# Reading the values' PSUM bank twice on ScalarE and making x's low part on Pool, in units 1 to 7

## The chip, the cores and the metric

The kernel runs on one core of a Trainium2 chip. The metric is the device time of one execution in microseconds (us), from the first to the last instruction with what lies around them; the profile gives the span of one execution, engine by engine.

## What is computed

Three blocks follow each other. Attention takes q, k and v of 4 batches, 8 heads, 768 positions and 64 values a head; every query sees 8 global keys and 96 local ones, with a bias that grows with the distance. Its output is laid out as x, 3072 tokens by 512. The first feed-forward block is dense, the second sends each token to one of eight experts. Cut to what matters here:

```python
attn_out = softmax(scale * q @ k.T + bias, masked) @ v
x = attn_out.transpose(0, 2, 1, 3).reshape(B * S, H * D)   # 3072 x 512
h = x @ w_in                                               # 512 x 2048
z = (h * cos(h)) @ w_out                                   # 2048 x 512
out = z, or for tokens with z @ w_skip > 0: z + gate * expert(z)
```

## The kernel before

**Units.** The 3072 tokens are eight units of 384 (UT), numbered 0 to 7. For each unit attention gives x transposed: four chunks of 128 rows (one pair of heads each, `p` = 0 to 3) by 384 tokens. The dense block needs x more exactly than one rounded operand, so x is held as two fp32r tiles, `xhi` (x rounded) and `xlo` (what is left), and each product is three matmuls: `wi_hi` by `xhi`, `wi_hi` by `xlo`, `wi_lo` by `xhi` (L516). The second product, `zp` (L555), does the same with `ghi`, `glo`, `wo_hi` and `wo_lo`.

**What runs beside what.** The attention of unit 0 comes first (up to about 53 us). After that `unit(u)` runs the dense block of unit u in 16 steps `f`, and the attention of unit u+1 is dealt out over its 32 slots (two a step, `HS`). Through unit 0's dense block the weights are converted as well (L212 to L264). In units 1 to 6 the first half of the slots also holds the routing scores of the unit before: 27 products on VectorE (DVE), `junk` L613. Unit 7 has no attention beside it; the experts follow.

**One pair of heads in the slots.** With s0 the first slot of pair p, scores come at s0, s0+1 and s0+2 (`att_S`, t = 0, 1, 2: two matmuls each into two PSUM banks `ps_s`, L394, each read by DVE at L399, which adds the bias and gives the minimum). The exponentials (L413, ScalarE) follow, then the scaling by Pool (L423), the transposes `ps_p` at s0+5 to s0+7 (copied out by ScalarE, L439 and L441, into `pT`), and at s0+9 the product with the values, `ps_v` (`att_V`, L450 and L455). As pairs are eight slots apart, `att_V` of one pair stands in the same slot as `att_S` t = 1 of the next, just ahead of it; t = 2 is one slot later.

**The banks.** From unit 1 on, `ps_s`, `ps_p` and `ps_v` take turns in three banks of the pool `ps_a` (one tag). Around `att_V` the turn is: `ps_v` in the first bank, the two products of t = 1 in the second and third, then the two products of t = 2 in the first (which `ps_v` must have left) and in the second (which L399 of t = 1, first head, must have read). In unit 0 the values' product is in a bank of another pool (`hp`).

**The values' bank before.** ScalarE rounds it into `xhi` (L464); DVE then reads it again and subtracts `xhi` (L465) to make `xlo`. The bank is free when L465 is done.

**Order on the engines.** TensorE's and ScalarE's instructions run in the order in which the program states them. DVE's and Pool's order is chosen by the framework's planner from its own estimates when the program is built, and each engine then keeps that order whatever is late. ScalarE's order in a step is: L488 (rounds the angle of `hp`), in an `att_V` step L464, then L504 (the sine, which waits for DVE's L499), then L526 (`ghi`). DVE's is L499, L542 (`r` times `hp`), L482 (`wi_lo`) with the attention's and the routing's work between. Pool makes `wi_hi` (L479) and `glo` (L527), and in unit 0's dense block also L230 of the conversion.

**The tile that the change takes.** `pT` has three buffers (`HT`), one for each t of a pair; they are read by the matmuls of `att_V`.

Of the kernel before, what the change touches and what calls it, by code (L numbers as in the profile page):

```python
# [9 lines left out]
F32 = mybir.dt.float32  # L10
# [5 lines left out]
ALU = mybir.AluOpType  # L16
# [4 lines left out]
P = 128  # L21
# [16 lines left out]
def kernel(  # L38
    ctx, tc, q, k, v, n_global, n_local, w_in, w_out, w_skip, w_gate, w1, w2, out
):  # L40
    nc = tc.nc
# [8 lines left out]
    HT = 3  # L50
    UT = HT * P
# [20 lines left out]
    ap_ = att_pool.enter_context(tc.tile_pool(name="ap", bufs=2))  # L72
# [12 lines left out]
        out=upper, in_=ones, pattern=[[1, P]], base=0, channel_multiplier=-1,  # L85
# [15 lines left out]
    for j, a in enumerate((n_global, n_local)):  # L101
# [11 lines left out]
        out=lim, in0=lim_h, scalar=2.0 ** 32, in1=lim, op0=ALU.mult, op1=ALU.add  # L113
# [19 lines left out]
        out=loc, in0=rel, scalar=nlo, in1=dst, op0=ALU.is_lt, op1=ALU.mult  # L133
# [14 lines left out]
    def to_far(d, kept):  # L148
# [12 lines left out]
        out=dst_f, in0=tmp, scalar=nlo, in1=dst[:, 104:NW], op0=ALU.mult, op1=ALU.add  # L161
# [6 lines left out]
        out=dst[:, 0:8], in0=g8[:, 0:8], scalar1=nlo, scalar2=None, op0=ALU.mult  # L168
# [170 lines left out]
    def att_ps(u, name):  # L339
        if u == 0:  # L340
            if name == "ps_v":
                return ps_h.tile([P, UT], F32, name="hp")
            return ps_z.tile([P, DM], F32, name="zp")
        return ps_a.tile([P, 512], F32, name=name, tag="ps")
# [98 lines left out]
    def att_V(u, p):  # L443
        d = att[u, p]
        av = att_ps(u, "ps_v")
        for t in range(HT):
            first, pt = u % 2 == 0 and t == 0, d["pt", t]
            if not first:
                for j in range(2):
                    nc.tensor.matmul(  # L450
                        av[j * D:(j + 1) * D, t * P:(t + 1) * P], d["va"][:, t, j, :],
                        pt[0:104, 0, j, :], start=True, stop=False,
                    )
            for j in range(2):
                nc.tensor.matmul(  # L455
                    av[j * D:(j + 1) * D, t * P:(t + 1) * P], d["v"][:, t, j, :],
                    pt[:, 1, j, :], start=first, stop=True,
                )
        if p == 0:
            att[u, "x"] = (  # L460
                mp.tile([P, CC, UT], F32R, name="xhi"), mp.tile([P, CC, UT], F32R, name="xlo")
            )
        xhi, xlo = att[u, "x"]
        nc.scalar.copy(xhi[:, p], av[:, 0:UT])  # L464
        nc.vector.tensor_tensor(  # L465
            out=xlo[:, p], in0=av[:, 0:UT], in1=xhi[:, p].bitcast(F32), op=ALU.subtract
        )


    gq = {}  # L470
# [251 lines left out]
    for u in range(1, NU):  # L722
        for p in range(NP):
            s0 = HS * (u - 1) + PS * p - 3
            at(s0 - 12, att_load, u, p)
            at(s0 - 5, att_load_v, u, p)
            at(s0 - 5, att_Tq, u, p)
            at(s0 - 4, att_Tk, u, p)
            for t in range(HT):
                at(s0 + t, att_S, u, p, t)  # L730
                at(s0 + 5 + t, att_P, u, p, t)
            at(s0 + 9, att_V, u, p)
            at(s0 + 2, att_load_va, u, p)
            at(s0 + 2, att_E, u, p, tail=True)
# [33 lines left out]
    for p in range(NP + 1):  # L768
        if p < NP:
            if p > 1:  # L770
                att_load_v(0, p)
            for t in range(HT):
                att_S(0, p, t)
            if p + 1 < NP:
                att_Tq(0, p + 1)
                att_Tk(0, p + 1)
            if p + 1 < NP:
                fill(p + 1)
            if p + 2 < NP:
                att_load(0, p + 2)  # L780
            att_E(0, p)
        warm(2, ps_a, "ps")
        if p > 0:
            for t in range(HT):
                att_P(0, p - 1, t)
            att_V(0, p - 1)
            if p < NP:
                att_load_va(0, p)
        conv_tick()
# [168 lines left out]
    with tc.manual_schedule(engines={mybir.EngineType.PE}):  # L958
# [8 lines left out]
        with tc.manual_schedule(engines={mybir.EngineType.SP}):  # L967
            with tc.manual_schedule(engines={mybir.EngineType.Activation}):


                u = NU - 1
# [72 lines left out]
                with tc.manual_schedule(engines={mybir.EngineType.Pool, mybir.EngineType.DVE}):  # L1044
                    with tc.manual_schedule(engines={mybir.EngineType.Activation}):
# [17 lines left out]
                        def trans_x0(cs):  # L1063
# [16 lines left out]
                            out=sel, in0=slots, scalar1=r.sf[:, 0], scalar2=None, op0=ALU.is_equal  # L1080
# [67 lines left out]
        out=ctl[:, 1:2], in0=ctl[:, 4:5], scalar1=float(NE), scalar2=None, op0=ALU.is_gt  # L1148
# [207 lines left out]
    with tc.If(reg(ctl_i[0:1, 1:2], 1) > 0):  # L1356
# [4 lines left out]
        with tc.tile_pool(name="gp", bufs=2) as gp:  # L1361
# [9 lines left out]
                out=nb[:, 0:E], in0=nb[:, 0:E], scalar1=1.0 / P,  # L1371
# [3 lines left out]
                out=nb[:, E:E + 1], in0=ctl[:, 0:1], scalar1=-float(NB0), scalar2=float(NB0),  # L1375
# [6 lines left out]
            for e in range(E):  # L1382
                nc.gpsimd.indirect_dma_start(
                    out=xs[:, :], out_offset=bass.IndirectOffsetOnAxis(ap=pi[:, e:e + 1], axis=0),
# [40 lines left out]
```

## Time and profile before

| | |
|---|---|
| runs, us | 1033.59, 1036.96, 1031.6 (median 1033.59) |
| profiled execution, us | 1035.09 |
| its span, us | 1033.3 |
| PE busy | 967.6 us, 94% |
| DVE busy | 740.2 us, 72% |
| Pool busy | 539.7 us, 52% |
| ScalarE busy | 528.2 us, 51% |
| mean granted TensorE clock | 0.967 |

Busy time is a sum over the whole span. A row of a timeline gives start, duration, engine, line and names; what stands in brackets is the idle time of that engine just before it and the instruction that ended it. PE is the matmul row, PEld the weight loads, ACT is ScalarE, POOL is Pool. One matmul of fp32 operands shows as two records.

### The profile page before, as it was taken

Reading aid. Unit: us, or ns where it says so; the run is one execution under the profiler, and the core shown is the slowest. Engines: PE = TensorE matmul, PEld = TensorE weight load, DVE = VectorE, ACT = ScalarE, POOL = GpSimd, SP = SyncE. Lnnn points to the kernel's source line nnn. Section 1 sums busy time; section 2 is a strip of 40 time slices with the busy share of each in tenths; the row PEclk is TensorE's granted clock in tenths of the full one; section 3 lists DMA queues with packets and bytes.
Section 4 is the critical chain, followed back from the end, with each engine's and each line's share of the span. In section 5 each row is a group of like instructions: output and inputs, shape, how many; then the busy total and the mean of one; then the engine's idle time right before and its main releaser. Section 6 shows DMA issues by size and latency. Waiting matters only on the chain.

```text
span 1033.3 us, 17028 instructions
## 1 busy us (share of the span) xinstructions
PE 967.6 (94%) x5673; PEld 814.5 (79%) x5677; DVE 740.2 (72%) x1835; ACT 528.2 (51%) x1279; POOL 539.7 (52%) x727
## 2 busy tenths in 40 slices
PE   8888888999999999999899999999999999999996
PEld 4577666878787887788788778877898789999995
DVE  6588887896698569658854975696474288888883
ACT  4676766656556565566576566656564111111110
POOL 3577767443454444454455445454555165656662
PEclk8889889999999999999999999999999989999998
DMA  7386764544554321122111211200004187556500
GB/s 184 88 228 181 209 179 148 162 120 138 144 142 132 103 63 28 34 54 69 28 40 40 58 28 41 67 12 17 12 31 181 37 322 267 198 203 222 196 25 21
DMA packets 141824, 115.07 MB, mean 111 GB/s; under 512 B 99735, under 2 KB 116119, under 8 KB 141600
## 3 DMA queue, kind: packets, MB, share of 16 engines
q1 hardware_dynamic: 138496, 107.89, 34.9%
q0 software_dynamic: 3200, 5.98, 1.5%
q8 instruction: 47, 0.77, 0.3%
q14 instruction: 49, 0.40, 0.1%
q10 hardware_dynamic: 32, 0.03, 0.0%
HBM read 97.36 MB, written 21.05 MB: 115 GB/s over the span
## 4 chain that ended last, share of the span: by engine, by line
PE 53%; DVE 25%; POOL 10%; issue 6%; ACT 3%; DMA 2%; POOLq 0%; SPq 0%; ACTq 0%; DVEq 0%
PE hp L516 13%; PE zp L555 13%; PE hp L933 9%; PE zp L952 9%; DVE junk L613 8%; DVE wi_lo L482 4%; POOL sc L423 4%; PE ps_s L394 3%; POOL wi_hi L479 2%; DVE r L499 2%; POOL glo L527 2%; DVE sc L399 2%; DVE r L542 2%; DVE w_in_sb L219 1%; DVE w_in_sb L223 1%
## 5 line engine op out<-in xcount | busy, mean ns | idle before, releaser
L527 POOL TENSOR_TENSOR glo<-r,ghi 128x384 fp32r<-128x384 f32 x115 | 130.9, 1138 | 198.1 <-ACT ghi L526 178.5
L516 PE MATMUL hp<-xhi,wi_hi 128*128 128x384 f32 x492 | 179.2, 364 | 4.6 <-DVE r L542 3.1
L482 DVE TENSOR_TENSOR wi_lo<-w_in_sb,wi_hi 128x512 fp32r<-128x512 f32 x124 | 108.0, 871 | 102.8 <-POOL wi_hi L479 100.2
L516 PE MATMUL hp<-xhi,wi_lo 128*128 128x384 f32 x492 | 168.5, 342 | 1.1 <-DVE wi_lo L482 1.1
L516 PE MATMUL hp<-xlo,wi_hi 128*128 128x384 f32 x492 | 168.0, 342 | 0.0
L555 PE MATMUL zp<-wo_hi,ghi 128*128 128x512 f32 x345 | 147.4, 427 | 0.4 <-ACT r_zr L575 0.4
L504 ACT ACTIVATE r<-r,halfpi 128x384 f32<-128x384 f32 x128 | 78.9, 617 | 132.9 <-DVE r L499 131.7
L555 PE MATMUL zp<-wo_lo,ghi 128*128 128x512 f32 x345 | 137.2, 398 | 3.9 <-DVE wo_lo L264 3.9
L613 DVE CUSTOM_DVE_ANT_0 junk<-r_zr,wrep 128x512 bf16<-128x512 f32 x162 | 135.5, 837 | 7.1 <-ACT r_zr L575 5.3
L555 PE MATMUL zp<-wo_hi,glo 128*128 128x512 f32 x345 | 136.8, 397 | 0.1
L423 POOL TENSOR_SCALAR sc<-sc,sm 128x232 f32<-128x232 f32 (+1 forms) x180 | 88.8, 513 | 70.1 <-DVE sm L418 59.1
L526 ACT CAST ghi<-r 128x384 fp32r<-128x384 f32 x115 | 59.0, 513 | 108.2 <-DVE r L542 107.6
L516 PEld LDWEIGHTS hp<-xhi,wi_hi 128*128 128x128 f32 x492 | 94.6, 192 | 20.0 <-issue 14.1
L479 POOL TENSOR_SCALAR wi_hi<-w_in_sb 128x512 fp32r<-128x512 f32 x128 | 92.0, 719 | 33.0 <-PE hp L516 26.1
L394 PE MATMUL ps_s<-kW,qT 64*128 64x232 f32 (+1 forms) x384 | 81.1, 415 | 27.7 <-DVE xlo L465 14.7
L938 ACT ACTIVATE hh<-hp 128x256 fp32r<-128x256 f32 x64 | 24.7, 386 | 149.3 <-PE hp L933 149.3
L516 PEld LDWEIGHTS hp<-xhi,wi_lo 128*128 128x128 f32 x492 | 94.4, 192 | 1.5 <-DVE wi_lo L482 1.4
L516 PEld LDWEIGHTS hp<-xlo,wi_hi 128*128 128x128 f32 x492 | 94.8, 193 | 0.2
L394 PEld LDWEIGHTS ps_s<-kW,qT 64*128 64x128 f32 x384 | 42.8, 197 | 62.0 <-DVE xlo L465 21.3
L413 ACT ACTIVATE sc<-sc,mx 128x232 f32<-128x232 f32 (+1 forms) x180 | 83.3, 464 | 6.1 <-DVE mx L399 4.8
L542 DVE TENSOR_TENSOR r<-r,hp 128x384 f32<-128x384 f32 x112 | 61.5, 549 | 31.6 <-ACT r L504 31.4
L871 POOL TENSOR_SCALAR w2h<-we 128x512 fp32r<-128x512 f32 x64 | 48.7, 760 | 67.3 <-PE zp L952 67.3
(234 smaller groups left out, 2266.6 us busy)
## 6 DMA issues: line engine op xcount, KB each, us to landing
we<-in_moe_w_dram SPq DMA_DIRECT2D x16, 2048.0 KB
st<-in_moe_w_in_dram SPq DMA_DIRECT2D x16, 512.0 KB
st<-in_moe_w_out_dram SPq DMA_DIRECT2D x16, 512.0 KB
ck<-in_moe_w_in_dram SPq DMA_DIRECT2D x16, 512.0 KB
ck<-in_moe_w_out_dram SPq DMA_DIRECT2D x16, 512.0 KB
ld_q<-in_q_dram SPq DMA_DIRECT2D x64, 96.0 KB
ld_k<-in_k_dram SPq DMA_DIRECT2D x64, 96.0 KB
ld_v<-in_v_dram SPq DMA_DIRECT2D x64, 96.0 KB
```

The costliest lines, as they stand in the source:

```text
L394: nc.tensor.matmul(sp[:, c0:NW], d["qT"][j * D:(j + 1) * D, t * P:(t + 1) * P], d["kW"][j * D:(j + 1) * D, t, c0:NW], start=True, stop=True,)
L413: nc.scalar.activation(out=s[:, j, c0:NW], in_=s[:, j, c0:NW], func=AF.Exp, scale=-1.0, bias=d["m"][:, t, j:j + 1], accum_out=sm[:, t, j:j ...
L423: nc.gpsimd.tensor_scalar(out=s[:, j, c0:NW], in0=s[:, j, c0:NW], scalar1=sm[:, t, j:j + 1], scalar2=1.0, op0=ALU.mult, op1=ALU.mult,)
L479: nc.gpsimd.tensor_scalar(out=hi, in0=ws, scalar1=1.0, scalar2=1.0, op0=ALU.mult, op1=ALU.mult)
L482: eng.tensor_tensor(out=lo, in0=ws, in1=hi.bitcast(F32), op=ALU.subtract)
L516: nc.tensor.matmul(hp, a[:, c, :], b[:, c, :], start=(n == 0), stop=(n == 3 * CC - 1))
L527: nc.gpsimd.tensor_tensor(out=glo, in0=r, in1=ghi.bitcast(F32), op=ALU.subtract)
L542: nc.vector.tensor_tensor(out=r, in0=r, in1=hp, op=ALU.mult)
L555: nc.tensor.matmul(zt[u][t], a[:, sl], b[:, f, :], start=(f == 0 and n == 0), stop=(f == FC - 1 and n == 2),)
L613: nc.vector.tensor_tensor_reduce(out=junk, in0=self.zr[:, t, 0:DM], in1=self.wrep[e], op0=ALU.mult, op1=ALU.add, scale=1.0, scalar=0.0, ac ...
L933: nc.tensor.matmul(hp, a[:, c, :], b[:, c, :], start=(n == 0), stop=(n == 3 * CC - 1))
L952: nc.tensor.matmul(yq[e][j], a[:, sl], b, start=(f == 0 and n == 0), stop=(f == F2C - 1 and n == 2),)
```

## The change

In units 1 to 7 ScalarE reads the values' bank a second time and copies it as it is into a new tile `xf`, which is taken from the buffers of `pT`. Pool subtracts `xhi` from `xf` to make `xlo`. In unit 0 all stays.

```diff
         xhi, xlo = att[u, "x"]
         nc.scalar.copy(xhi[:, p], av[:, 0:UT])
-        nc.vector.tensor_tensor(
-            out=xlo[:, p], in0=av[:, 0:UT], in1=xhi[:, p].bitcast(F32), op=ALU.subtract
-        )
+        if u == 0:
+            nc.vector.tensor_tensor(
+                out=xlo[:, p], in0=av[:, 0:UT], in1=xhi[:, p].bitcast(F32), op=ALU.subtract
+            )
+        else:
+
+            xf = ap_.tile([P, 2, 2, P], F32, name="pT", bufs=HT)
+            xf = xf.rearrange("p a b c -> p (a b c)")[:, 0:UT]
+            nc.scalar.copy(xf, av[:, 0:UT])
+            nc.gpsimd.tensor_tensor(out=xlo[:, p], in0=xf, in1=xhi[:, p].bitcast(F32), op=ALU.subtract)
```

## Rows read from the trace of the kernel before

**Rows 1.** The page, busy time of each engine and its share of the span.
```profile
PE 967.6 (94%) x5673; PEld 814.5 (79%) x5677; DVE 740.2 (72%) x1835; ACT 528.2 (51%) x1279; POOL 539.7 (52%) x727
```
**Rows 2.** Busy time by stretch: length, PE, PEld, DVE, ACT, POOL, then clock, DMA.
```profile
70.00:162.00 92.00, 78.18 (x404) 63.02 (x402) 76.17 (x133) 60.67 (x139) 68.82 (x72) 0.89 0.67 189
...
540.00:634.00 94.00, 90.64 (x542) 76.14 (x541) 66.28 (x199) 58.33 (x143) 45.91 (x69) 1.00 0.17 42
...
573.00:583.00 10.00, 9.41 (x63) 7.54 (x62) 9.46 (x30) 5.04 (x11) 3.92 (x4) 1.00 0.14 32
```
**Rows 3.** DVE's read of the values' bank, and TensorE's wait for the bank.
```profile
L465 DVE TENSOR_TENSOR xlo<-ps_v,xhi x28: 543/551/554, 77.4 to 742.9; 128x384 fp32r<-128x384 f32 x28
...
PE ps_s L394: 14.7, 14
```
**Rows 4.** Waits, units 1 to 6 (162 to 729 us): total, times, longest.
```profile
POOL glo L527 <- ACT ghi L526: 174.2, 66, 5.6
...
ACT r L504 <- DVE r L499: 91.9, 59, 3.3
...
PE ps_s L394 <- DVE xlo L465: 10.4, 11, 1.2
```
**Rows 5.** Waits, unit 0's dense block (70 to 162 us): total, times, longest.
```profile
PE ps_s L394 <- DVE xlo L465: 4.3, 3, 3.3
```
**Rows 6.** Timeline around one stop of TensorE in unit 5.
```profile
574.35 1.25 POOL L527 TENSOR_TENSOR glo<-r,ghi 128x384 fp32r<-128x384 f32 x1 [4.05 <-PE hp L516]
...
574.78 1.37 DVE L613 CUSTOM_DVE_ANT_0 junk<-r_zr,wrep 128x512 bf16<-128x512 f32 x1
...
575.44 0.66 PE L394 MATMUL ps_s<-kW,qT 64*128 64x232 f32 x4
...
575.56 0.48 ACT L464 CAST xhi<-ps_v 128x384 fp32r<-128x384 f32 x1 [0.71 <-PE ps_v L455]
...
575.57 1.06 POOL L479 TENSOR_SCALAR wi_hi<-w_in_sb 128x512 fp32r<-128x512 f32 x1
...
576.66 0.69 DVE L482 TENSOR_TENSOR wi_lo<-w_in_sb,wi_hi 128x512 fp32r<-128x512 f32 x1 [0.51 <-POOL wi_hi L479]
...
577.74 0.68 DVE L613 CUSTOM_DVE_ANT_0 junk<-r_zr,wrep 128x512 bf16<-128x512 f32 x1
...
577.86 0.62 ACT L504 ACTIVATE r<-r,halfpi 128x384 f32<-128x384 f32 x1 [1.81 <-DVE r L499]
...
578.35 0.55 DVE L465 TENSOR_TENSOR xlo<-ps_v,xhi 128x384 fp32r<-128x384 f32 x1
...
578.82 0.39 DVE L399 CUSTOM_DVE_ANT_0 sc<-ps_s,bias_n 128x232 f32<-128x232 f32 x1
...
578.96 0.97 PE L394 MATMUL ps_s<-kW,qT 64*128 64x232 f32 x4 [0.59 <-DVE xlo L465]
```
**Rows 7.** Single lines over the run: duration in ns, least/median/most.
```profile
L613 DVE CUSTOM_DVE_ANT_0 junk<-r_zr,wrep x162: 649/692/1496, 186.0 to 698.1; 128x512 bf16<-128x512 f32 x162
...
L482 DVE TENSOR_TENSOR wi_lo<-w_in_sb,wi_hi x124: 676/693/1787, 24.7 to 781.7; 128x512 fp32r<-128x512 f32 x124
...
L527 POOL TENSOR_TENSOR glo<-r,ghi x115: 989/1017/1549, 62.4 to 791.7; 128x384 fp32r<-128x384 f32 x115
```
**Rows 8.** Timeline around a values' product in the second half of unit 5.
```profile
624.38 0.48 ACT L464 CAST xhi<-ps_v 128x384 fp32r<-128x384 f32 x1 [0.71 <-PE ps_v L455]
...
624.95 0.40 DVE L399 CUSTOM_DVE_ANT_0 sc<-ps_s,bias_n 128x232 f32<-128x232 f32 x1
625.04 0.62 ACT L504 ACTIVATE r<-r,halfpi 128x384 f32<-128x384 f32 x1 [0.19 <-DVE r L499]
...
625.27 0.55 DVE L465 TENSOR_TENSOR xlo<-ps_v,xhi 128x384 fp32r<-128x384 f32 x1
...
626.06 0.55 DVE L542 TENSOR_TENSOR r<-r,hp 128x384 f32<-128x384 f32 x1
```
**Rows 9.** Timeline around the longest stop, in unit 0's dense block.
```profile
103.30 0.47 ACT L464 CAST xhi<-ps_v 128x384 fp32r<-128x384 f32 x1
...
109.94 1.45 PE L394 MATMUL ps_s<-kW,qT 64*128 64x232 f32 x4 [3.29 <-DVE xlo L465]
```

## The prediction

> **What bounds the kernel now.** I read the busy times first. TensorE is busy for 94% of the span [rows 1], and in a unit with routing for 90.64 of 94 us [rows 2]: what can be won in units 1 to 6 is some 3 us a unit, plus what hides in stretched matmuls. Unit 0's dense block is different: TensorE is busy for 78.18 of 92 us while DVE has 76.17 and Pool 68.82 [rows 2]. Then I read the values' bank. TensorE stops 14 times, 14.7 us in all, for a bank that `ps_v` holds until DVE's L465 is done [rows 3]; 10.4 us of it lie in units 1 to 6 [rows 4] and 4.3 us in unit 0's dense block [rows 5]. That sum is the prize in sight.
>
> One such stop shows what it is made of [rows 6]. ScalarE has rounded the bank at 576.04, but DVE comes to L465 only at 578.35, because it is full: 9.46 us of the 10 around it [rows 2]. It ends at 578.90 and TensorE goes on at 578.96. What matters is the next row: L399 of t = 1 stands right behind L465 in DVE's queue, at 578.82 to 579.21. TensorE's t = 2 has two products, and only the first waits for `ps_v`. The second needs the bank that this L399 reads. The pair took 0.97 us here and 0.66 where nothing held it at 575.44, so the second did wait, by some 0.31 us. **The bank is one lock, DVE's queue the second, 0.3 us behind it.** In the second half of a unit, where no routing runs, DVE reaches L399 first and L465 within 0.9 us of L464 [rows 8], and TensorE does not stop: about half of the 28 products with values have no stop at all.
>
> **The change part by part.** The sum is made against the profiled execution: 1035.09 us, a span of 1033.3 and 1.8 around it, 1.5 above the median of the runs (1033.59). I take differences from it to the median.
>
> *Removed from DVE:* 28 times L465, 0.55 us each [rows 3], 15.4 us busy. The instruction behind it started 0.47 us after it [rows 6], so L399 moves up by 0.47 us where DVE is late. At 14 stops that is 6.6 us at most. The first product of t = 2 gains more, but it then waits with TensorE for the second, so the rest of the 14.7 us is not won by this term.
>
> *Added to ScalarE:* 28 copies of 128x384 out of PSUM. The trace has no such plain copy of this bank; L464 reads the same bank at the same size in 0.48 us, and I take that: 13.4 us. It stands ahead of L504, which waits for DVE's L499: 1.81 us in the stop [rows 6], 91.9 us in all over units 1 to 6 [rows 4]. In the unhurried place that cover is only 0.19 us [rows 8], so L504 would start about 0.3 us later and end at 625.95 in place of 625.66; L542, which waits for it, started at 626.06, and stays. Cost nothing; without cover it would be 0.3 to 0.48 us for each of some 14 places, 7 us at the outside, on a chain whose next user is two steps later.
>
> *The bank:* free two reads after L464 starts, about 1.0 us, in place of 3.3 [rows 6] or 6.6, where TensorE stood for 3.29 us, the longest stop of all [rows 9]. The first lock is gone everywhere, and L399 is late next.
>
> *Added to Pool:* 28 subtractions of 128x384 from two SBUF tiles, the form of L527, at 1.02 us (0.99 to 1.55) [rows 7]: 29 us. In units 1 to 6 Pool waits 174.2 us for `ghi` [rows 4], and the new instruction falls into that gap, after L479, where it stood idle for 4.05 us at a time [rows 6]. The first user of `xlo` is the next unit's product, after at least one whole step. In unit 0's dense block Pool has 23 us free in 92 [rows 2], four instructions of about 1.3 us need 5. Where one falls ahead of an L479, `wi_hi` is late and DVE's L482 behind it. Bounds for the three stops there [rows 5]: 0 where it falls into a gap, 1.3 us each where the whole instruction is in front, 0 to 4 us. I take 0.3 each, nearer the gap, as Pool has one free for each.
>
> *What Pool's instruction does to DVE:* before, L465 had one input in PSUM and took 543 to 554 ns whatever ran beside it [rows 3]. L613, with two inputs in SBUF, took 0.68 us alone at 577.74 and 1.37 beside Pool's L527 and L479 at 574.78 [rows 6]; L613 spans 0.65 to 1.50 us and L482 0.68 to 1.79 [rows 7]. The new instruction is ready at 576.52 and Pool is free at 576.63, just as L482 starts at 576.66, two instructions ahead of the L399 that TensorE needs. So what L399 wins by 0.47, it loses by up to 0.68 (1.37 - 0.69). The stops of units 1 to 6, 12 with those where only the weight load waited, repeat the pattern of rows 6 with the DVE work shifted. In seven the new instruction falls wholly onto an L613 or L482, and I charge 0.62; in five it falls partly onto L499, whose `hp` is in PSUM, and I charge 0.4: an estimate of 0.52 on average. That gives 12 x (0.52 - 0.47) = +0.6 us. With no contention it is 12 x -0.47 = -5.6; with the full 0.68 it is +2.5. In unit 0 the DVE work between (L223, L482) is of the same kind: -0.47 + 0.5 + 0.3 = +0.3 a stop, three stops, +0.9 (bounds -1.4 to +4).
>
> A page's rule is harder. The Trainium skill, "SBUF — State Buffer", section "Who interferes with whom", says that a DVE instruction with two SBUF inputs and a GpSimd instruction that reads SBUF block each other fully, whoever issued second waiting out the first. The rows show L613 stretched by 0.69 us beside Pool's instructions, which overlapped it nearly throughout. By the rule the terms above would be up to 1.02 a stop; by the row they are 0.52.
>
> *The buffer:* `xf` takes the turn of `pT` for t = 0, whose readers are the matmuls that L464 waits for anyway; the next pair's t = 2 then waits for Pool, six slots later. Nothing.
>
> **Sum:** +0.6 (twelve stops of units 1 to 6) and +0.9 (unit 0's dense block) make +1.5. At the 14 places without a stop DVE has as much less to do, 14 x 0.47 = 6.6 us, and loses most of it again to Pool; an estimate of 0.1 us of each, 1.5 us, comes through where routing follows. That leaves 0 against the median: 1033.6 us. A measurement of this kernel can tell about 0.5%, 5.2 us, from no change.
>
> **The rivals.**
>
> *Faster: the planner also moves L399 up.* Where DVE has L399 ahead, as in rows 8, TensorE does not stop. If, with L465 gone, the planner puts L399 of t = 1 ahead of the routing's L613 (the one at 577.74 stood ahead of it [rows 6]), both locks open and the 14.7 us go but for some remainder: 10 to 14 us, 1020 to 1024. If it only loses the contention that I charge, 6.6 us: 1027. For it: the order is chosen anew. Against it: L399 stands right behind L465 in the stop, with the L613 ahead of both [rows 6], and nothing in the change makes L399 ready sooner. Chance 0.23 for both.
>
> *Slower: Pool's read holds DVE for its whole length.* Place: the routing halves and unit 0, where Pool's instruction starts with or before an L613, L482 or L223. Price: 1.02 - 0.47 = 0.55 us at each of 14 stops, 7.7 us, and about 1 from Pool's queue in unit 0: 1042. It decides from the point where the stretch of DVE at the stops is over 0.85 us on average (0.47 and 5.2/14). For it: L482 goes up to 1.79 us [rows 7], that is 1.1 over its least. Against it: L613's 1.37. Chance 0.14. The rule of the Trainium skill named above ("SBUF — State Buffer", "Who interferes with whom") is this case.
>
> *Slower: Pool's queue order.* If the planner puts the subtraction ahead of L479, `wi_hi` waits for `xf` (576.52 for 575.57 in the stop) and for 1.02 us more, 2 us, and DVE's L482 and all behind it wait too. At twelve stops, with half of it caught by slack, 12 us: 1046. Against it: L479 started at 575.57, a microsecond before `xf` would be there [rows 6]. Chance 0.05.
>
> *It does not open the bank.* If the second read stood behind other work on ScalarE, the bank would be free no sooner and DVE still relieved: no change either. Program order puts it right behind L464. Chance 0.03, counted under no change.
>
> **How the numbers follow.** No change within 0.5%: 0.55 + 0.03 = 0.58. Faster by more: 0.23. Slower by more: 0.14 + 0.05 = 0.19. Low 1026 takes in the 1027 of the contention-free case and leaves out the planner's 10 to 14 us (about 0.1); high 1041 takes in contention between the row's and the full length and leaves out the rest of the slower cases (about 0.1).
>
> **What would show it.** Right: no stop of L394 for `xlo` or `xf`; in the routing halves a stop of L394 for L399 (`mx`) of 0.5 to 1.2 us in its place; L613, L482 of over 1.2 us beside Pool's new row; DVE's busy time down by less than 15.4 us; Pool up by 29 to 35, ScalarE by 13. Wrong on the fast side: L399 within 2 us of L464 in the routing halves, and no stop there. Wrong on the slow side: L482 waiting for L479 longer, or L613 near 1.7 us.

## The result, and the profile after

The change made the kernel slower: median 1044.72 us against 1033.68 for the kernel before on the same chip, a ratio of 1.0102 over all runs (95% interval 1.0081 to 1.0122; it is not the quotient of the two medians). The forecast was no change, at 1033.6 us (1026 to 1041). Measured once more beside the experiments it came to 1.0080 (1.0050 to 1.0111). The profiled execution took 1043.59 us, with a span of 1041.8 us.

The page's busy times, for [rows 1]:

```profile
PE 973.4 (93%) x5677; PEld 816.1 (78%) x5677; DVE 737.4 (71%) x1807; ACT 538.5 (52%) x1307; POOL 569.8 (55%) x755
```

Pool is up by 30.1 us, as 28 subtractions should make it, and ScalarE by 10.3 rather than 13, as each copy's row begins about 0.1 us before that of L464 has ended. DVE lost 28 instructions of 0.55 us, 15.4 us, and is down by only 2.8. The two new lines have the forecast durations, 0.49 and 1.02 us (single lines, least/median/most in ns):

```profile
L473 ACT COPY pT<-ps_v x28: 481/487/496, 74.7 to 749.1; 128x384 f32<-128x384 f32 x28
L474 POOL TENSOR_TENSOR xlo<-pT,xhi x28: 987/1017/1500, 77.4 to 749.7; 128x384 fp32r<-128x384 f32 x28
```

Where DVE's gain went stands in one line: L482 of before is L489 now (lines of before from 475 on are 7 higher). First the kernel before, then the change (the page's groups: total busy, mean ns):

```profile
L482 DVE TENSOR_TENSOR wi_lo<-w_in_sb,wi_hi 128x512 fp32r<-128x512 f32 x124 | 108.0, 871 | 102.8 <-POOL wi_hi L479 100.2
```
```profile
L489 DVE TENSOR_TENSOR wi_lo<-w_in_sb,wi_hi 128x512 fp32r<-128x512 f32 x124 | 118.0, 952 | 110.6 <-POOL wi_hi L486 109.9
```

The same 124 instructions take 10.0 us more. In the waits, TensorE no longer stops for `xlo` (14.7 us in [rows 3]); it stops for L399, where before it did so 9 times for 5.0 us:

```profile
PE ps_s L394 <- DVE mx L399: 20.9, 20, 3.4
```

One stop of unit 5, the counterpart of [rows 6] (timeline of the change):

```profile
578.68 0.48 ACT L464 CAST xhi<-ps_v 128x384 fp32r<-128x384 f32 x1 [0.41 <-PE ps_v L455]
...
579.06 0.49 ACT L473 COPY pT<-ps_v 128x384 f32<-128x384 f32 x1
...
579.19 1.05 POOL L486 TENSOR_SCALAR wi_hi<-w_in_sb 128x512 fp32r<-128x512 f32 x1
...
580.22 1.02 POOL L474 TENSOR_TENSOR xlo<-pT,xhi 128x384 fp32r<-128x384 f32 x1
580.28 1.50 DVE L489 TENSOR_TENSOR wi_lo<-w_in_sb,wi_hi 128x512 fp32r<-128x512 f32 x1 [0.50 <-POOL wi_hi L486]
...
582.17 0.68 DVE L620 CUSTOM_DVE_ANT_0 junk<-r_zr,wrep 128x512 bf16<-128x512 f32 x1
...
582.78 0.39 DVE L399 CUSTOM_DVE_ANT_0 sc<-ps_s,bias_n 128x232 f32<-128x232 f32 x1
...
583.23 0.66 PE L394 MATMUL ps_s<-kW,qT 64*128 64x232 f32 x2 [1.15 <-DVE mx L399]
```

The bank is free at 579.55. But Pool's subtraction and DVE's `wi_lo` both stand behind the same `wi_hi`, so they start together, at 580.22 and 580.28. Pool's ends at 581.24, and `wi_lo` ends 0.54 us after that: it took 1.50 us, where in [rows 6] it took 0.69. L399 starts 2.50 us after `wi_lo` does; in [rows 6] it was 2.16 (578.82 - 576.66), with L465 still between. The stop is longer than before.

By unit, most of the difference lies in one place. From one first rounding of an angle (L488, now L495) to that of the next unit, unit 6 takes 95.97 us in the change, 96.10 in its second profile and 91.06 before; the five units before it take 0.4 us more on average. Around unit 6's stop (timeline of the change):

```profile
699.16 0.47 ACT L464 CAST xhi<-ps_v 128x384 fp32r<-128x384 f32 x1
...
700.40 2.65 POOL L486 TENSOR_SCALAR wi_hi<-w_in_sb 128x512 fp32r<-128x512 f32 x3
...
703.03 0.99 POOL L474 TENSOR_TENSOR xlo<-pT,xhi 128x384 fp32r<-128x384 f32 x1
703.06 1.00 DVE L649 TENSOR_TENSOR r_ex<-r_lg,r_mx 128x24 f32<-128x24 f32 x1
...
704.14 0.68 DVE L489 TENSOR_TENSOR wi_lo<-w_in_sb,wi_hi 128x512 fp32r<-128x512 f32 x1
704.74 0.39 DVE L399 CUSTOM_DVE_ANT_0 sc<-ps_s,bias_n 128x232 f32<-128x232 f32 x1
...
705.19 1.14 PE L394 MATMUL ps_s<-kW,qT 64*128 64x232 f32 x2 [2.67 <-DVE mx L399]
```

The planner has put the routing's choice (`r_mx` to `r_m`) and two `wi_lo` ahead of L399 here, and Pool's read holds one of the choice's small instructions for a microsecond (`r_ex` takes 0.17 where nothing runs beside it). TensorE stops for 2.67 us, where before it stopped for 1.22. And its clock falls, from the last microsecond of the stop on. Busy times by stretch of the change (length, PE, PEld, DVE, ACT, POOL, granted clock, DMA):

```profile
704.00:708.00 4.00, 2.81 (x7) 2.24 (x8) 3.35 (x16) 2.02 (x3) 1.38 (x4) 0.51 0.00 0
708.00:712.00 4.00, 4.00 (x16) 3.72 (x16) 1.00 (x4) 3.96 (x15) 0.62 (x1) 0.63 0.00 0
```

0.51 is close to the lower of its two levels, 1.2 GHz for 2.4. In the kernel before, all of 700 to 720 us is at 1.00. The two stretches together fall 4 x 0.49 + 4 x 0.37 = 3.4 us short of full clock. About 0.5 us of that lies before 705.19, while TensorE still stood (from 704.00 to 705.19 the granted clock is 0.54); the other 2.9 and the 1.45 us by which the stop is longer make 4.3 of the 4.9 us by which unit 6 is longer.

### The profile page after: what moved, and what is told of

Read it like the earlier page. It is cut to its first block, busy times and chain, and to the rows that moved or that the text cites. A ratio compares the mean times of both kernels' runs of the same rounds, so it can differ in the third digit from the quotient of the medians.

```text
span 1041.8 us, 17072 instructions
## 1 busy us (share of the span) xinstructions
PE 973.4 (93%) x5677; PEld 816.1 (78%) x5677; DVE 737.4 (71%) x1807; ACT 538.5 (52%) x1307; POOL 569.8 (55%) x755
## 5 line engine op out<-in xcount | busy, mean ns | idle before, releaser
L489 DVE TENSOR_TENSOR wi_lo<-w_in_sb,wi_hi 128x512 fp32r<-128x512 f32 x124 | 118.0, 952 | 110.6 <-POOL wi_hi L486 109.9
L394 PE MATMUL ps_s<-kW,qT 64*128 64x232 f32 (+1 forms) x384 | 85.6, 415 | 26.7 <-DVE mx L399 20.9
L394 PEld LDWEIGHTS ps_s<-kW,qT 64*128 64x128 f32 x384 | 42.8, 197 | 64.1 <-DVE mx L399 29.6
L562 PEld LDWEIGHTS zp<-wo_hi,ghi 128*128 128x128 f32 x345 | 66.1, 192 | 20.7 <-issue 7.8
```

The lines of the kernel that those rows point to most:

```text
L394: nc.tensor.matmul(sp[:, c0:NW], d["qT"][j * D:(j + 1) * D, t * P:(t + 1) * P], d["kW"][j * D:(j + 1) * D, t, c0:NW], start=True, stop=True,)
L489: eng.tensor_tensor(out=lo, in0=ws, in1=hi.bitcast(F32), op=ALU.subtract)
L562: nc.tensor.matmul(zt[u][t], a[:, sl], b[:, f, :], start=(f == 0 and n == 0), stop=(f == FC - 1 and n == 2),)
```

## The experiments

Four theories. **A**: Pool's read of two SBUF tiles holds up DVE just ahead of L399. **B**: the planner's other order on DVE costs the time, above all in unit 6. **C**: ScalarE's second read delays what stands behind it. **O**: Pool is busier, so `wi_hi` and `glo` come late.

**One part at a time.** First the subtraction back on DVE, from the copy, which takes Pool out and leaves the second read and the early bank:

```diff
-            nc.gpsimd.tensor_tensor(out=xlo[:, p], in0=xf, in1=xhi[:, p].bitcast(F32), op=ALU.subtract)
+            nc.vector.tensor_tensor(out=xlo[:, p], in0=xf, in1=xhi[:, p].bitcast(F32), op=ALU.subtract)
```

> ScalarE copies the bank as in the change, but DVE subtracts, from the copy. Theory A (Pool's reading of two SBUF tiles holds up DVE's L482 and L613 just ahead of L399): with Pool's instruction gone the slowdown goes; DVE keeps its subtraction but no longer at the head of the stop, so 1028 to 1034 us. Theory B (the planner's new DVE order in units 4 and 6, the routing's choice and two early wi_lo ahead of L399, costs most): that order is not taken here, 1030 to 1034, so A and B agree on this run. Theory C (ScalarE's second copy delays the sine and the exponentials): still slow, 1040 to 1045.

Measured: 1.0008 (0.9991 to 1.0024), with a median of 1035.76 us a little above the range, and far from C's. Then the kernel before with ScalarE's copy added and read by nobody (DVE still reads the bank):

```diff
+        if u > 0:
+            xf = ap_.tile([P, 2, 2, P], F32, name="pT", bufs=HT)
+            xf = xf.rearrange("p a b c -> p (a b c)")[:, 0:UT]
+            nc.scalar.copy(xf, av[:, 0:UT])
```

> The kernel before plus ScalarE's second read of the bank, its copy unread; DVE subtracts from the bank as before, so the bank is freed by DVE. Theories A and B: the copy stands in time ScalarE waits anyway, 1032 to 1036 us, with the stops for xlo still there (about 15 us on TensorE). Theory C: 1040 to 1045.

Measured: 1.0030 (1.0009 to 1.0050). That lies between the forecasts. DVE's planned order is not that of the kernel before here, so whether the 0.3% is the copy's or the order's stays open; in the run before it the same copy costs nothing that can be told. Then DVE's subtraction from the copy, three slots later for p = 0 to 2, so that L399 has neither the bank nor L465 ahead of it:

```diff
-            nc.gpsimd.tensor_tensor(out=xlo[:, p], in0=xf, in1=xhi[:, p].bitcast(F32), op=ALU.subtract)
+            att[u, p]["xf"] = xf
+            if p == NP - 1:
+                att_lo(u, p)
...
+    def att_lo(u, p):
+        xhi, xlo = att[u, "x"]
+        xf = att[u, p]["xf"]
+        nc.vector.tensor_tensor(out=xlo[:, p], in0=xf, in1=xhi[:, p].bitcast(F32), op=ALU.subtract)
...
+            if p < NP - 1:
+                at(s0 + 12, att_lo, u, p)
```

> ScalarE copies the bank; for pairs 0 to 2 DVE subtracts from the copy three slots after the values' product, for pair 3 at once. Nothing of Pool's is added and L465 is out of DVE's way ahead of L399. Theory A: the whole 0.47 us at each of 14 stops comes in, 1025 to 1030 us. Theory B: no early wi_lo ahead of L399 in unit 6, the same 1025 to 1031. If neither the bank nor L399 is what holds TensorE: 1033.

Measured: 0.9989 (0.9970 to 1.0008). The wait for `xlo` is gone, that for L399 is 11.5 us in 17 stops, 8 us less than the two together before (14.7 and 5.0), and the time is the same, not the 1025 to 1030 us that was expected. The prize in sight was not to be had. In its profile other waits grew (L435 for Pool's scaling from 5.4 to 6.5 us) and unit 1 is 3.1 us longer; but the profiled execution, 1038.34 us, is the slowest of its twelve (median 1033.36).

**The read alone.** Pool's subtraction replaced by a fill of `xlo` (x's low part is left out, here and in the next run of this kind); DVE's planned order is the change's to the last instruction:

```diff
-            nc.gpsimd.tensor_tensor(out=xlo[:, p], in0=xf, in1=xhi[:, p].bitcast(F32), op=ALU.subtract)
+            nc.gpsimd.memset(xlo[:, p].bitcast(F32), 0.0)
```

> As the change, with DVE's queue in the same order, but Pool fills xlo with zeros in place of the subtraction, so it reads nothing from SBUF and is done at other times: x's low part is left out of the result. Theory A: at the stops L482 is back to 0.69 us from 1.49 and L399 is 0.8 us earlier; 12 stops by 0.8 is 10 us less than the changed kernel, 1033 to 1037, with the 4 us of unit 6 still there. Theory B: the order of DVE's queue is the same, so at most 2 or 3 us come back, 1040 to 1044.

Measured: 0.9979 (0.9958 to 1.0000). The fills ran at other times than the subtractions, which left Pool's being busy at that moment as a cause. So came a repetition of the change,

> The changed kernel again, on the chip of the three runs beside it, so that they are compared with it there. 1042 to 1047 us; in unit 6 the stop at the second pair again about 2.7 us, that unit some 4 to 5 us longer than in the kernel before.

(measured: 1.0080, 1.0050 to 1.0111) and two runs with DVE's order again unchanged. The subtraction issued twice:

```diff
+            nc.gpsimd.tensor_tensor(out=xlo[:, p], in0=xf, in1=xhi[:, p].bitcast(F32), op=ALU.subtract)
```

> The change with Pool's subtraction issued twice in a row; DVE's order is that of the change. Theory A (Pool's reading holds up DVE): the second meets what DVE does next, L613 or L399's neighbours, 0.3 to 0.7 us more at some 14 stops, 1048 to 1054 us. Theory O (not the reading but Pool's time counts, by late wi_hi and glo): Pool has some 4 us free at these places, 1044 to 1047.

And in its place two fills of `xf`, which only write:

```diff
-            nc.gpsimd.tensor_tensor(out=xlo[:, p], in0=xf, in1=xhi[:, p].bitcast(F32), op=ALU.subtract)
+            nc.gpsimd.memset(xf, 0.0)
+            nc.gpsimd.memset(xf, 0.0)
+            nc.gpsimd.memset(xlo[:, p].bitcast(F32), 0.0)
```

> The change with Pool's subtraction replaced by two fills of the copied tile with zeros at the same place of Pool's queue (they must wait for ScalarE's copy too) and xlo filled with zeros: x's low part is left out. Pool is as busy as in the change or longer, writes, and reads nothing from SBUF. DVE's order is that of the change. Theory A: L482 is back at 0.69 us, 1031 to 1036 us. Theory O: 1043 to 1047, as the change.

Measured: twice 1.0183 (1.0154 to 1.0212; its median of 1055.59 us is above even A's range), write-only 0.9986 (0.9963 to 1.0008). The stop of unit 5 in the write-only run (timeline):

```profile
573.58 0.41 POOL L474 MEMSET pT<- 128x384 f32 x1
...
573.67 0.69 DVE L491 TENSOR_TENSOR wi_lo<-w_in_sb,wi_hi 128x512 fp32r<-128x512 f32 x1 [0.51 <-POOL wi_hi L488]
...
574.05 0.42 POOL L475 MEMSET pT<- 128x384 f32 x1
...
575.35 0.40 DVE L399 CUSTOM_DVE_ANT_0 sc<-ps_s,bias_n 128x232 f32<-128x232 f32 x1
...
575.81 0.66 PE L394 MATMUL ps_s<-kW,qT 64*128 64x232 f32 x2 [0.32 <-DVE mx L399]
```

Pool works at the same moment, and `wi_lo` takes its 0.69 us. L399 starts 1.68 us after `wi_lo`, in the change 2.50, before 2.16: the removed L465 gives 0.48 and the read takes 0.82. The same place with the subtraction twice:

```profile
587.93 1.01 POOL L474 TENSOR_TENSOR xlo<-pT,xhi 128x384 fp32r<-128x384 f32 x1
...
588.00 1.50 DVE L490 TENSOR_TENSOR wi_lo<-w_in_sb,wi_hi 128x512 fp32r<-128x512 f32 x1 [0.51 <-POOL wi_hi L487]
...
589.02 1.33 POOL L475 TENSOR_TENSOR xlo<-pT,xhi 128x384 fp32r<-128x384 f32 x1
...
589.88 1.02 DVE L621 CUSTOM_DVE_ANT_0 junk<-r_zr,wrep 128x512 bf16<-128x512 f32 x1
```

The second one holds `junk` as well, 1.02 for 0.68 us. One read costs 0.8%, two cost 1.8%, a Pool that only writes nothing: O and C are out, and B alone is too, as DVE's order is the same in all four. Both runs with fills also feed TensorE zeros as x's low part; that this is not what gives the time back is seen from the two runs with DVE's subtraction, which feed it the true values and are at 1.0008 and 0.9989. The Trainium skill, "SBUF — State Buffer", section "Who interferes with whom", says just this: two SBUF inputs on DVE contend with a GpSimd instruction that reads SBUF, not with one that only writes. The trace agrees, 1.50 against 0.69 us.

**Where it costs.** The old path for two of the 28, so that the planner no longer orders unit 6 as above:

```diff
-        if u == 0:
+        if u == 0 or (u, p) in ((7, 0), (6, 3)):
```

> The change without it in two of the 28 places (pair 3 of unit 6, pair 0 of unit 7), which gives a DVE order in unit 6 with the routing's choice and the two early wi_lo behind L399. Theory A alone: 26/28 of the slowdown stays, 1043 to 1045 us. Theory A with B (the order of that one stop costs 4 us of the 10): 1039 to 1041, unit 6 about 91 to 92.5 us long in place of 96.

Measured: 1.0043 (1.0024 to 1.0062). In its profile unit 6 takes 90.91 us, as before: a third to a half of the loss hangs on one place (by the medians 5.5 of 7.8 us are left, by the ratios 0.43 of 0.80%). Then the same reads moved away from L399's neighbours, first by stating the subtraction three slots later for p = 0 to 2, as above but on Pool:

```diff
+        nc.gpsimd.tensor_tensor(out=xlo[:, p], in0=xf, in1=xhi[:, p].bitcast(F32), op=ALU.subtract)
```

> Pool still subtracts 28 times from the copy, the same two SBUF tiles in the same 1.02 us, but for p = 0 to 2 three slots after the values' product (the place that the late subtraction of DVE had), for p = 3 at once. By A what costs is the place: Pool's read beside the wi_lo that stands ahead of the L399 TensorE waits for. Moved away from there the 21 later ones hold up DVE work that nobody waits for: 1035 to 1038 us, 0.0 to +0.3%, the waits of L394 for L399 at 10 to 14 us in place of 20.9, and about 28 to 32 of the 124 wi_lo over 1.2 us. And as the granted clock fell behind the lengthened stops, the time by which it falls short of 1.00 from 160 us on comes down from 8.6 to 10.3 us (the two profiles of the change) to some 3 to 5 (before 3.4). If Pool's reading costs wherever it runs (DVE's total is the bound), or if a busier Pool does (O), it stays at 1042 to 1045, +0.7 to +1.0%.

Measured: 1.0085 (1.0064 to 1.0105), but this moved nothing: the planner issued Pool's subtraction as soon as its operands were there, beside the same `wi_lo` (1.50 us in unit 5), and TensorE's stops are those of the change. It counts as a third measurement of the change. Then held in place by a tiny in-order copy on ScalarE:

```diff
+        if p < NP - 1:
+            nc.scalar.copy(xf[:, 0:8], xf[:, 0:8])
         nc.gpsimd.tensor_tensor(out=xlo[:, p], in0=xf, in1=xhi[:, p].bitcast(F32), op=ALU.subtract)
```

> The late subtraction on Pool again, now held there: for p = 0 to 2 ScalarE first copies eight columns of the copy onto themselves at the slot of the subtraction (the run before, without that, had Pool's subtraction back beside the same wi_lo, because the planner moves it up as soon as its operands are there). By A the stops of p = 0 to 2 in units 1 to 6 lose Pool's read ahead of L399: wi_lo there back to 0.69 us, L394's waits for L399 at 10 to 14 us in place of 20.4, the granted clock's shortfall from 160 us on at 3 to 6 us in place of 12, and 1034 to 1038 us, 0 to +0.3%; some other DVE instruction is held up for each read, which nobody waits for. If the read costs wherever it runs, 1042 to 1045 as in the change.

Measured: 1.0089 (1.0063 to 1.0115). A as stated falls: the read does not cost only beside that `wi_lo`. TensorE's 120 products (240 records) of t = 0 to 2 with 232 columns between 162 and 745 us, and what they waited for, in the change and in this run (lines by form: busy, mean ns, idle before, with what ended it):

```profile
L394 PE MATMUL ps_s<-kW,qT 64*128 64x232 f32 x240 | 52.6, 410 | 15.9 <-DVE mx L399 12.9 <-ACT pT L441 2.8
```
```profile
L394 PE MATMUL ps_s<-kW,qT 64*128 64x232 f32 x240 | 53.7, 408 | 15.0 <-DVE mx L399 7.6 <-ACT pT L441 7.3
```

The wait for L399 fell as expected, from 12.9 to 7.6 us; a wait for ScalarE's copies out of `ps_p` took its place. Unit 4 shows why (timeline of this run):

```profile
499.51 1.46 POOL L484 TENSOR_TENSOR xlo<-pT,xhi 128x384 fp32r<-128x384 f32 x1
...
500.02 1.50 DVE L629 CUSTOM_DVE_ANT_0 junk<-r_zr,wrep 128x512 bf16<-128x512 f32 x1
...
501.57 0.97 DVE L629 CUSTOM_DVE_ANT_0 junk<-r_zr,wrep 128x512 bf16<-128x512 f32 x1
...
502.47 0.55 DVE L515 SCALAR_TENSOR_TENSOR r<-r,hp 128x384 f32<-128x384 int32 x1
...
504.86 0.51 ACT L542 CAST ghi<-r 128x384 fp32r<-128x384 f32 x1 [1.19 <-DVE r L558]
...
505.54 0.38 ACT L441 COPY pT<-ps_p 104x256 f32<-104x256 f32 x1
...
505.97 0.66 PE L394 MATMUL ps_s<-kW,qT 64*128 64x232 f32 x2 [2.27 <-ACT pT L441]
```

Now the read holds `junk` (1.50 for 0.68 us) ahead of `r`; the sine and `ghi` come later, and ScalarE's copies stand behind `ghi` in its queue. In the kernel before the same stop is 0.88 us:

```profile
502.61 0.66 PE L394 MATMUL ps_s<-kW,qT 64*128 64x232 f32 x2 [0.88 <-ACT pT L441]
```

Not all of the 1.39 us between them is the read's, which is 0.8: the planner has also put a second `junk` ahead of `r`, the one of 0.97 us. So a read can cost at other places as well, where DVE is full; how much of this run's 0.9% the reads make, and how much its own order and ScalarE's 21 small copies, is not shown. Last, the change by halves:

```diff
-        if u == 0:
+        if u < 2 or p < 2:
```

> The change only for p = 2 and 3 of units 2 to 7 (12 of the 28 subtractions), whose bank is read in the second half of a unit, where no routing runs on DVE; the other 16 as before. The run with the held subtraction has shown that the narrow form of A (only beside the wi_lo ahead of L399) does not hold: the wait came back on ScalarE's copies behind DVE's r. The wide form: a Pool read holds DVE for its length wherever DVE is full, that is in the routing halves and in unit 0. By it these 12 cost nothing: 1033 to 1037 us, -0.2 to +0.2%. If each of the 28 costs alike, 12 of them make +0.36% (1038.5 us).

```diff
-        if u == 0:
+        if u == 0 or u > 1 and p > 1:
```

> The other 16: the change only for all of unit 1 (read in unit 0's dense block) and for p = 0 and 1 of units 2 to 7 (read in the routing halves). By the wide form of A nearly the whole of the change's +0.85%: 1040 to 1045 us, +0.6 to +1.0%. If each costs alike, +0.49% (1040). As the planner's order around L399 differs from the change's in some stops, by half a per cent either way at the outside, B alone would show as a result that follows neither.

Measured: the 12 reads outside the routing halves 1.0038 (1.0024 to 1.0053), the other 16 1.0076 (1.0056 to 1.0096). The 16 carry nearly the whole loss, as the wide form of A says. The 12 should have been free and were not; 0.38% is what "each costs alike" gave (0.36%). Their profile speaks against it: beside ten of the 12 reads every DVE instruction keeps its length (most are L399, L506 and L549, which have an operand in PSUM), and only two reads hold a `wi_lo`, for 0.80 us each. In the profile of the other 16, nine reads hold a `wi_lo` and two a `junk`, 7.2 us in all. What the profile of the 12 does have is two new places, both of the planner's making. In unit 6 it put the choice and a `wi_lo` ahead of DVE's own `xlo` (a stop of 2.25 us, then a granted clock of 0.64 in 704 to 708 us), with no new Pool read there: that unit is 3.5 us longer. In unit 1, 3.7 us longer, it put the routing's indirect DMA ahead of `wi_hi` on Pool:

```profile
269.00 1.00 POOL L692 DMA_INDIRECT xs<-r_zr,r_si  x1 [3.19 <-PE ps_s L394]
...
270.69 1.49 DVE L489 TENSOR_TENSOR wi_lo<-w_in_sb,wi_hi 128x512 fp32r<-128x512 f32 x1 [5.87 <-POOL wi_hi L486]
...
273.01 0.81 PE L394 MATMUL ps_s<-kW,qT 64*128 64x232 f32 x2 [1.29 <-DVE mx L399]
```

Units 2 to 5 together are 1.0 us shorter than before. That the 12 reads themselves are nearly free is what this one profile suggests; it was not measured without the planner's part. The halves add up to more than the whole; each has its own order, which may be why.

No version beat both kernels: the best that computes everything, DVE's late subtraction, cannot be told from the kernel before.

## Why the prediction was wrong

**Right.** The bank opens and no stop of L394 for `xlo` or `xf` is left. L399 is late next, with stops of 0.5 to 1.2 us in most of the routing halves (the three longest there are 1.27, 1.64 and 2.67). ScalarE's copy (0.49 us) and Pool's subtraction (1.02 us) have the forecast sizes, and the buffer and C cost nothing that shows beside them. DVE's busy time is down by less than 15.4 us. The 0.47 us that L399 was to gain is there once the read is away (0.48 in the write-only run).

**The step that failed: "What Pool's instruction does to DVE".** It charged 0.52 us a stop, from an L613 of 1.37 us beside Pool's L527 in [rows 6], 0.69 over its length alone. That row shows only a remainder: L527 had started at 574.35, 0.43 us ahead of it. It ended at 575.60, and L613 ran for another 0.55 us until 576.15. Read so, DVE had waited for the whole rest of Pool's instruction, and an instruction that starts together with Pool's would wait for its whole length. The new one does start together with `wi_lo`, since both wait for the same `wi_hi`; the rows had that too (L479 ends at 576.63, L482 starts at 576.66). Measured, it is +0.80 to +0.82. The rival "Pool's read holds DVE for its whole length", to which I gave 0.14, is what happened; against it I had set only that 1.37. It costs 0.8 and not 1.02 because `wi_lo` starts 0.06 us late and needs only 0.54 us behind Pool's end in place of 0.69.

I could have read that price off the kernel before. There Pool's L527, of the form and the length of the new subtraction, starts 0.07 us or so ahead of a `wi_lo` in 20 places, and each of these takes 1.47 to 1.50 us and ends 0.55 us after L527. One of them (timeline of the kernel before):

```profile
591.44 1.01 POOL L527 TENSOR_TENSOR glo<-r,ghi 128x384 fp32r<-128x384 f32 x1
...
591.51 1.49 DVE L482 TENSOR_TENSOR wi_lo<-w_in_sb,wi_hi 128x512 fp32r<-128x512 f32 x1 [0.95 <-POOL wi_hi L479]
```

With 0.81 in place of 0.52 the prediction's own sum for the twelve stops is 12 x (0.81 - 0.47) = +4.1 us in place of +0.6. That is close to the 4.5 to 5.5 us that are left where unit 6 has its old order, but it makes only some 1037 us, inside the stated range; the rest of the loss needs the two terms that follow. (The sum also counts one values' product too many: 12, 3 and 14 make 29 of 28, worth 0.1 us.)

**A term that was missing: the order.** I let the planner's new order speak on the fast side alone. It did move L399 up in two places, in units 3 and 5, after 415.55 and 605.32 us, where stops of 1.19 and 1.22 us went (the two times are those of L464 in the change); but at the second values' product of unit 6 it put the choice ahead of L399. With that order and no read there the stop is 1.84 us in both runs with fills, and unit 6 takes 91.93 us in the write-only one and 93.11 in the other; with the read, 2.67 and 95.97. First the kernel before, then the write-only run:

```profile
699.28 0.97 PE L394 MATMUL ps_s<-kW,qT 64*128 64x232 f32 x4 [1.22 <-DVE xlo L465]
```
```profile
696.46 0.66 PE L394 MATMUL ps_s<-kW,qT 64*128 64x232 f32 x2 [1.84 <-DVE mx L399]
```

Without that order a third to a half of the loss is gone. Order and read come together there, and the rival's own price, 14 x 0.55 us, came near the right sum partly by luck.

**Another: the clock behind a stop.** I priced stops by their length. Over the timed runs the mean granted clock is 0.9712 in the kernel before (24 runs), 0.9670 in the change repeated (7), 0.9600 with the subtraction twice (6) and 0.9723 in the write-only run (12). The first two differ by 0.0042, which over 1042 us is at most 4.4 us (less where TensorE stood anyway), up to about half of the 7.8 between their medians. It isn't needed for every loss: the profiled execution of the held subtraction took 1042.65 us at a mean granted clock of 0.972, though over its six runs the mean is 0.968.

**The prize.** Without any contention I put the gain at 5.6 us. Both runs without a Pool read gave 0.9979 and 0.9986, intervals that reach from -0.4% to +0.1%, while TensorE's waits for L399 and the bank fell from 19.7 to 11.6 and 12.9 us. So stops that are 7 to 8 us shorter brought some 1 to 2 us by the medians. In the two profiles unit 6, with its new order, took back 0.9 and 2.1 us; where the rest went is not shown.

## What to carry to other kernels

Before work is moved from a full DVE to an idle Pool, look at what both wait for: if one producer releases Pool's new two-input instruction and a DVE instruction with two SBUF inputs, they start together and DVE waits for Pool's whole length, here 0.8 us to save 0.47. A row stretched by contention tells only what was left of the other engine's instruction; look up when that one began and ended, and look in the trace for a pair that starts together. Where the DVE instructions beside Pool's read have an operand in PSUM, as beside most reads in the second half of a unit here, nothing was held. Where a planner sets the order, compare the planned order around each stop before pricing a change of one instruction, as one unlucky place was worth a third to a half of this result.

## What the runs showed of the hardware

- A DVE instruction with both inputs in SBUF did not run slower beside Pool's subtraction; it waited for the end of it. `wi_lo` ended 0.54 us after Pool's subtraction did, and a 128x24 instruction of 0.17 us took 1.00. It goes the other way too: a subtraction that started just behind a `junk` (294.58 and 294.52 us in the change) took 1.50 us for 1.02. Two fills of 0.41 and 0.42 us by Pool at the same place left `wi_lo` at 0.69.
- DVE instructions with an operand in PSUM were not held: of those that lay beside Pool's subtraction for over 0.2 us in the change, 21 of L399 took 0.39 to 0.40 us, seven of L506 0.54 to 0.55 and five of L549 0.54 to 0.56, as elsewhere.
- Around the end of a stop of TensorE of 2.67 us the granted clock was 0.51 and 0.63 in two stretches of 4 us, and after one of 1.15 us, at 583.23 us, it was 0.58 in one such stretch, which is 1.7 us short of full clock. So a stop can cost more behind its end than within it. Not every one did: after the stops of 1.14 us at 247.36 and of 1.64 us at 514.37 no stretch of 4 us fell below 0.97. The same stop of 1.84 us in unit 6 was followed by 1.00 in the write-only run and by 0.76 and 0.81 in the other run with fills.
